# A written instruction order that ends with the first unit is continued to the end of the second

## The chip, the cores and the metric

The kernel runs on one core of a Trainium2 chip. Its engines have queues of their own, each worked off in order: PE (TensorE, matmuls and transposes), DVE (VectorE), ACT (ScalarE), POOL (GpSimd) and SP (SyncE, which here only issues DMA loads). The metric is the device time in microseconds (us). Three runs of the kernel before gave 574.34, 570.67 and 573.80 us, median 573.8.

## The reference

A windowed attention, a gated feed-forward layer and a layer of eight experts with a balanced assignment follow each other; 2 batches of 768 tokens, 8 heads of 64, model width 512:

```python
k_sum = k.reshape(B, H, nb, block, D).max(axis=3)      # block 32, nb 24
v_sum = v.reshape(B, H, nb, block, D).mean(axis=3)
scores_l = where(|i - j| < 16, scale * q @ k.T, -1e9)  # window
scores_s = scale * q @ k_sum.T + log(block)            # block means
a = softmax(concat([scores_l, scores_s]))
x = a @ concat([v, v_sum])

h = x @ w_in                                           # 512 -> 2048
x = (h * clip(h + 3, 0, 6) / 6) @ w_out                # 2048 -> 512
# then: logits x @ w_gate, each expert takes its 192 best tokens, relu(x @ w1) @ w2
```

## The kernel before

**Tiles and units.** The 1536 tokens are 12 tiles of 128; tiles 0 to 5 are batch 0 and 6 to 11 batch 1. Three tiles make a unit, so units 0 and 1 are batch 0, units 2 and 3 batch 1. A tile is worked on in two halves of four heads, numbered 0 to 23 (half 12 is the first of tile 6). The first layer's product of a unit is 16 slices (`gemm1_slice`, L684 to L686) of 12 matmuls of 384 columns each. Slices take turns in two PSUM banks (5 and 6), so a slice can start only when the slice two before it has been read out by ACT and DVE.

**One half of attention** goes through all engines: scores on PE (L423), mask and minimum on DVE (L433), exponentials on ACT (L439), norms on DVE (L443, L444), scaling on POOL (L448), transposes on PE (L470), their copy on ACT (L475), values on PE (L492). Behind a tile's second half stand its high part on ACT (L504) and its low part on DVE (L509). Per tile there are also the turning of the queries (PE L384, ACT L389) and the window of keys (DVE L406). Three buffers `Abuf` carry the halves, so about two are under way at once.

**Once per batch** the keys are turned into `kT` (for batch 1: six groups of four transposes, L368, each with a copy on ACT, L370, and a maximum over blocks on DVE, L371). The means of the values over blocks take POOL additions (L202 in three steps for batch 1, L209 for batch 0), a matmul (L217) and three copies (L221). The six key loads of batch 1 (256 KB each) go into four buffers `k1`, so the last two can be issued only when the first two groups have been turned.

**The weights** of the first layer arrive as 64-bit floats: a load of 512 KB per slice (L269), three integer operations on DVE (L295), a high part on ACT (L313) and a low part on POOL (L316).

**The order of the work.** `FIRST` is a list of short names written by hand, one per step, and `first_unit` runs them one after the other. The names that matter here are, by engine: PE: `K`/`Q` turn keys and queries of the start, `F` scores, `U` transposes, `V` values, `QP` turned queries, `M` means, `G` slices of unit 0, `N` filler matmuls on `ident`; DVE: `T` mask, `S` norms, `W` window, `c` weight conversion, `XL`; ACT: `E` exponentials, `C`, `X`, `H`, `EV` (read-out of a slice), `PL` (copies of the means); POOL: `P` scaling, `B` additions, `L` low weights; SP: `k`, `q`, `v`, `w`, `vw`, `kb`, `qq`, `vb` loads (the ones with `b` are batch 1's keys and values). Before, `FIRST` covers unit 0's slices and the attention of units 0 and 1 (tiles 0 to 5), and it ends there.

From then on `drive` mixes generators: for `u` = 1, 2, 3 it merges `gemm1(u)`, whose steps count 1950 each, with `attend_unit(u + 1)`, which draws steps from `halves()`; each stream moves in proportion to what it has done of its total (`ATTS[u + 1]` for the attention, spread over -0.02 to 0.92 of the stage). Before, `halves()` starts with tile 6: it issues the additions of batch 1's values, then all of `kprep`, the queries and the window, and then the halves. The stage of `u` = 1 ends when tile 8 is finished; by then the two fronts of tile 9 have also been issued, since halves lag by two.

The attention's share of a stage before, and the read-out of a slice, in the few lines:

```python
st = [[attend_unit(u + 1), ATTS[u + 1], -0.02, END[u]]]
drive([[gemm1(u), G1, 0, 1]] + st, soon)

p = gemm1_slice(u, f)
ACT.activation(T[u][:, f, :], p, AF.Relu, bias=three)
soon.append(partial(gate, T[u][:, f, :], p))
```

Of the kernel before, what the change touches and what calls it, by code (L numbers as in the profile page):

```python
# [12 lines left out]
OP = mybir.AluOpType  # L13
# [41 lines left out]
k00 k01 k10 k11 q0 q1 v0 w0 v1 vw0 w1 w2 w3 vw2 qq3 vw1 K001 K000 KE001 KR001 K010 KE000 KR000 K011 KE010 KR010  # L55
KE011 KR011 K100 KM0 K101 KE100 KR100 W0a KE101 K110 KR101 K111 KE110 KR110 KE111 Q01 KR111 Q00 QE01 KM1 W0b
QE00 Q11 Q10 QE11 F0 QE10 T0 E0 B0 N2 F1 T1 E1 S0 W1 P0 N3 M0 S1 c0_0 P1 c0_1 F2 B1 U0 c0_2 C0 T2 w4 qq4 H0 N1
U1 E2 F3 L0 M1 T3 C1 S2 W2 P2 E3 c1_0 F4 U2 PL2 c1_1 T4 C2 PL0 S3 N2 F5 c1_2 P3 PL1 W3 V0 U3 E4 T5 V1 c2_0 vw3
w5 X0 S4 c2_1 P4 E5 XL0 c2_2 N5 QP_3 C3 S5 H2 U4 c3_0 P5 H1 V2 c3_1 L2 C4 V3 c3_2 QE_3 U5 L1 X1 c4_0 V4 C5 XL1
F6 H3 c4_1 V5 L3 T6 QP_4 vw5 w6 w7 qq5 X2 E6 XL2 F7 c4_2 G0 W4 QE_4 H4 T7 L4 E7 G1 c5_0 S6 c5_1 P6 EV0 F8 EV1 S7  # L60
c5_2 P7 G2 T8 w9 w8 H5 E8 L5 c6_0 F9 c6_1 G3 EV2 W5 c6_2 U6 S8 EV3 c7_0 P8 H6 G4 T9 C6 L6 E9 c7_1 U7 c7_2 QP_5
w11 w10 EV4 S9 P9 C7 G5 c8_0 H7 c8_1 QE_5 L7 c8_2 U8 EV5 H8 c9_0 G6 L8 c9_1 c9_2 F10 EV6 w13 w12 vw4 H9 G7 T10
E10 L9 c10_0 c10_1 F11 EV7 S10 V6 c10_2 P10 G8 T11 w14 C8 H10 c11_0 E11 L10 c11_1 U9 c11_2 G9 EV8 S11 w15 kb0
kb1 kb2 kb3 qq6 vb0 vb1 H11 c12_0 P11 c12_1 L11 V7 EV9 c12_2 G10 vw6 qq7 C9 c13_0 H12 c13_1 X3 L12 c13_2 V8 EV10
# [34 lines left out]
def build(ctx, tc, q, k, v, w_in, w_out, w_gate, w1, w2, out):  # L99
# [30 lines left out]
    def bank(i):  # L130
        return psum.tile([128, 512], FT, name=f"bank{i}")
# [67 lines left out]
    def vsum(b):
        m = KR // 2  # L200
        while m:
            POOL.tensor_tensor(vs[:, :, :m], vs[:, :, :m], vs[:, :, m:2 * m], op=OP.add)  # L202
            m //= 2
# [7 lines left out]
    def vsum_mul(rows):  # L211
        means.append(bank(4))
        for i in rows:
            vsum_more(i, i == rows[0], i == rows[-1])

    def vsum_more(i, first, last):
        PE.matmul(means[-1][:KEYS], zones, vs[:, :, i], start=first, stop=last)  # L217

    def vsum_place(i):
# [87 lines left out]
        return win32[s % 4] if s < NF else wout32[(s - NF) % 3]  # L307

    def w_high(s):
        if s % 2 == 0:  # L310
            for _ in w_tiles(s):
                pass
        ACT.activation(WH[s], w_source(s), AF.Copy)  # L313

# [45 lines left out]
        ACT.activation(qT0[:, 2 * g + j].rearrange("p (s r) -> p r s", r=UT),  # L360
                       qps[g, j][:, :U].rearrange("p (r s) -> p r s", r=UT), AF.Copy)

    def kprep(b):
        for j in range(S // 128):
            x = raw.pop(("kraw", b, j))
            p = bank(2 + j % 2)
            for hp in range(HP):
                PE.transpose(p[:, hp * 128:(hp + 1) * 128],  # L368
                             x[:, 2 * hp:2 * hp + 2, :].rearrange("p h d -> p (h d)"), ident)
            ACT.activation(kT[:, :, :, 16 * j:16 * j + 16], p.rearrange("p (h s r) -> p h r s", h=HP, r=KR), AF.Copy)  # L370
            DVE.tensor_reduce(ks[:, :, 4 * j:4 * j + 4], p.rearrange("p (h n r) -> p h n r", h=HP, r=BLK),  # L371
                              axis=AX.X, op=OP.max)
            if b and j + 4 < S // 128:
                soon.append(partial(load_rows, "kraw", k, b, j + 4))
            yield 450
# [150 lines left out]
    pend, finished = [], set()  # L526

    def halves():
        for n in range(2 * UT, NT):
            b, i = divmod(n, 6)  # L530
            if i == 0:
                vsum(b)
                yield from kprep(b)
                q_prep(n)
                window(n)
                yield 2400
            for h in range(2):
                t = pend.pop(0) if len(pend) >= LAG else None
                if t:
                    turn(*t)  # L540
                    turned.append(t)
                    yield 660
                after = h == 1 and i < 5
                front(n, h, after)
                yield 1250 + 450 * after
                pend.append((n, h))
                while turned:
                    if turned[0] == (6 * b, 0):
                        vsum_mul([0])
                        for j in range(3):  # L550
                            vsum_place(j)
# [812 lines left out]
```

## Time and profile before

| | before |
|---|---|
| runs | 574.34, 570.67, 573.80 us |
| profiled execution, its own time | 573.23 us |
| its span, first to last instruction | 571.5 us |
| PE busy | 546.8 us, 96% |
| DVE, ACT, POOL busy | 360.7 (63%), 295.0 (52%), 168.1 us (29%) |
| start to the first slice of unit 0 | 0 to 41.1 us |
| unit 0's slices, with the attention of unit 1 | 41.1 to 85.6 us |
| unit 1's slices, with the attention of unit 2 | 85.6 to 146.3 us |
| unit 2's slices, with the attention of unit 3 | 146.3 to 191.1 us |
| the rest | 191.1 to 571.5 us |

The profiled time is 1.7 us longer than its span. Busy time counts an engine's own instructions. Matmuls overlap, so the time from one start to the next tells more of PE than the sum of their durations. A wait is put down to what released it.

### The profile page before, as it was taken

To read this page: it belongs to the slowest core of one execution; us is meant where nothing else is said; L and a number is where in the kernel's file an instruction comes from. 1 tells how busy PE (TensorE), PEld (TensorE's weight loads), DVE (VectorE), ACT (ScalarE), POOL (GpSimd) and SP (SyncE) were. 2 spreads that over 40 slices of the span, in tenths; PEclk is the share of its full clock that TensorE was granted. 3 is DMA by queue.
4 is the path that set the end of the run, shared out by engine and by line. 5 is a ranking of instruction groups with operands and counts; after the bars stand their busy time and mean duration, and the time that the engine had idled before them with its cause. 6 is when DMAs were issued, how large, how long until landed. Compare 5 with 4: busy or idle time off the path is not lost.

```text
span 571.5 us, 10909 instructions
## 1 busy us (share of the span) xinstructions
PE 546.8 (96%) x3901; PEld 459.8 (80%) x3901; DVE 360.7 (63%) x1036; ACT 295.0 (52%) x702; POOL 168.1 (29%) x198
## 2 busy tenths in 40 slices
PE   8889997899999999999999999998999999999993
PEld 8579896788989989866777777786888988998892
DVE  6799834445577786710165554543687888888870
ACT  4797643665544454732232322334567677676760
POOL 1646535112011232742254344463001110111011
PEclk9999998999999999999999999999999999999998
DMA  9996994122100453500070000025589987998701
GB/s 223 256 196 202 244 207 103 34 48 47 26 2 2 144 184 120 173 1 1 2 219 1 0 2 1 0 97 180 159 243 283 276 239 245 269 280 236 244 30 33
DMA packets 98271, 75.06 MB, mean 131 GB/s; under 512 B 38112, under 2 KB 84704, under 8 KB 98208
## 3 DMA queue, kind: packets, MB, share of 16 engines
q1 hardware_dynamic: 96224, 67.96, 44.0%
q0 software_dynamic: 1984, 6.32, 3.0%
q8 instruction: 33, 0.54, 0.4%
q14 instruction: 30, 0.25, 0.1%
HBM read 67.55 MB, written 6.71 MB: 130 GB/s over the span
## 4 chain that ended last, share of the span: by engine, by line
PE 56%; issue 27%; POOL 5%; DVE 4%; ACT 3%; DMA 2%; POOLq 0%; SPq 0%; DVEq 0%
PE bank L684 7%; PE bank L815 7%; PE bank L686 7%; PE bank L685 6%; PE bank L816 6%; PE bank L817 6%; POOL out_dram L1167 3%; PE bank L423 2%; PE bank L492 2%; POOL xs L748 2%; PE bank L726 2%; PE bank L470 2%; ACT A L439 2%; PE bank L638 1%; PE bank L335 1%
## 5 line engine op out<-in xcount | busy, mean ns | idle before, releaser
L684 PE MATMUL bank<-x,wh 128*128 128x384 f32 x256 | 91.6, 358 | 1.3 <-DVE t L714 1.3
L325 DVE TENSOR_TENSOR wl<-t,wh 128x1024 fp32r<-128x1024 f32 x64 | 77.0, 1221 | 20.5 <-ACT wh L324 18.7
L686 PE MATMUL bank<-x,wl 128*128 128x384 f32 x256 | 86.3, 337 | 0.0
L792 ACT ACTIVATE thx<-t 128x384 fp32r<-128x384 f32 (+2 forms) x80 | 36.0, 458 | 96.7 <-PE bank L816 89.3
L685 PE MATMUL bank<-x,wh 128*128 128x384 f32 x256 | 85.9, 336 | 0.0
L815 PE MATMUL bank<-wh,thx 128*128 128x512 f32 x192 | 79.4, 414 | 1.1 <-ACT thx L792 1.1
L793 POOL TENSOR_TENSOR tlx<-t,thx 128x384 fp32r<-128x384 f32 (+1 forms) x56 | 56.0, 1001 | 77.3 <-ACT thx L792 70.7
L817 PE MATMUL bank<-wh,tlx 128*128 128x512 f32 x192 | 75.4, 393 | 0.6 <-DVE tlx L793 0.5
L816 PE MATMUL bank<-wl,thx 128*128 128x512 f32 x192 | 75.0, 391 | 0.0
L1192 PE MATMUL bank<-x,wh 128*128 128x384 f32 x256 | 73.7, 360 | 0.5 <-DVE x L1118 0.5
L324 ACT ACTIVATE wh<-t 128x1024 fp32r<-128x1024 f32 x64 | 65.6, 1047 | 0.0
L1194 PE MATMUL bank<-x,wl 128*128 128x192 f32 x256 | 64.2, 251 | 0.0
L694 ACT ACTIVATE t<-bank,three 128x384 f32<-128x384 f32 x48 | 27.9, 581 | 65.4 <-PE bank L686 65.3
L1167 POOL DMA_INDIRECT out_dram<-t,idx x16 | 14.9, 931 | 141.5 <-DVE t L1216 136.0
L684 PEld LDWEIGHTS bank<-x,wh 128*128 128x128 f32 x256 | 48.3, 189 | 4.7 <-DVE t L714 2.2
L448 POOL TENSOR_TENSOR A<-A,sm 128x480 f32<-128x480 f32 x24 | 24.4, 1018 | 89.2 <-ACT at L475 41.9
L1194 PEld LDWEIGHTS bank<-x,wl 128*128 128x128 f32 x256 | 48.9, 191 | 0.3
L1192 PEld LDWEIGHTS bank<-x,wh 128*128 128x128 f32 x256 | 48.1, 188 | 1.2 <-DVE x L1118 0.8
L1208 PE MATMUL bank<-wh,t 128*128 128x512 f32 x128 | 48.9, 391 | 0.0
L685 PEld LDWEIGHTS bank<-x,wh 128*128 128x128 f32 x256 | 48.5, 189 | 0.0
L686 PEld LDWEIGHTS bank<-x,wl 128*128 128x128 f32 x256 | 48.2, 188 | 0.0
L815 PEld LDWEIGHTS bank<-wh,thx 128*128 128x128 f32 x192 | 36.0, 188 | 12.0 <-issue 2.9
(202 smaller groups left out, 1033.1 us busy)
## 6 DMA issues: line engine op xcount, KB each, us to landing
t<-in_moe_w_dram SPq DMA_DIRECT2D x128, 256.0 KB
t<-in_moe_w_in_dram SPq DMA_DIRECT2D x16, 512.0 KB
big<-in_moe_w_out_dram SPq DMA_DIRECT2D x16, 512.0 KB
VW<-in_v_dram SPq DMA_DIRECT2D x20, 192.0 KB
t<-in_v_dram SPq DMA_DIRECT2D x4, 768.0 KB
raw<-in_q_dram SPq DMA_DIRECT2D x9, 256.0 KB
t<-xs SPq DMA_DIRECT2D x8, 258.0 KB
t<-in_k_dram SPq DMA_DIRECT2D x4, 384.0 KB
```

Of the source, the lines that this page charges most:

```text
L324: ACT.activation(hi, x, AF.Copy)
L325: DVE.tensor_tensor(lo, x, hi.bitcast(FT), op=OP.subtract)
L684: PE.matmul(p, wh[:, kk, :], xh[:, kk, :], start=kk == 0, stop=False)
L685: PE.matmul(p, wh[:, kk, :], xl[:, kk, :], start=False, stop=False)
L686: PE.matmul(p, wl[:, kk, :], xh[:, kk, :], start=False, stop=kk == KD - 1)
L793: (DVE if placed[0] else POOL).tensor_tensor(ths[i][1], t, ths[i][0].bitcast(FT), op=OP.subtract)
L815: PE.matmul(acc[j], th[:, c], WH[s], start=f == 0, stop=False)
L816: PE.matmul(acc[j], th[:, c], WL[s], start=False, stop=False)
L817: PE.matmul(acc[j], tl[:, c], WH[s], start=False, stop=f == NF - 1)
L1192: PE.matmul(p, a[:, kk, :], xt[:, kk].rearrange("p c s -> p (c s)"), start=kk == 0, stop=False, skip_group_check=True)
L1194: PE.matmul(p[:, :CAP], b[:, kk, :], xt[:, kk, 0, :], start=False, stop=kk == KD - 1, skip_group_check=True)
L1208: PE.matmul(p, x, w, start=m == 0 and i == 0, stop=m == NM - 1 and i == 2)
```

## The change

`FIRST` goes on behind the last slice of unit 0. It now also holds unit 1's 16 slices (`Y`, read out by `YE` and gated by `GT`), batch 1's key groups (`KT` on PE, `KX` on ACT, `KN` on DVE), its means (`VS0` to `VS2` on POOL, `MB` on PE, `PB` on ACT), the queries of tiles 6 to 9, the halves 12 to 17, and the loads of tiles 6 to 11. Inside the part that was written before, many steps stand elsewhere too. `drive` begins at `u` = 2, and `halves()` at tile 9, with nothing under way, so the two fronts of tile 9 are issued there. Two of the eight filler matmuls at the start are gone. The sum of work is otherwise the same.

```diff
-ATTS = [0, 0, 26868, 18414]
+ATTS = [0, 0, 0, 21366]
 FIRST = """
...
+U11 VS0 G14 C11 V11 EV14 G15 X5 XL5 VS1 KT1 EV15 Y0 kb5 qq6 KN1 KX1 VS2 QP_7 YE0 KT3 GT0 KT0 KX3 KN3 Y1 kb4 vw8
+KX0 KN0 KT5 YE1 Y2 KN5 KX5 GT1 KT2 YE2 QP_6 KN2 KX2 Y3 qq8 qq9 QE_6 GT2 KT4 YE3 Y4 KN4 KX4 GT3 W6 MB YE4 GT4 Y5
+PB0 PB1 F12 PB2 Y6 T12 YE5 E12 GT5 F13 YE6 S12 QP_8 T13 P12 QE_7 Y7 E13 GT6 W7 S13 U12 YE7 P13 GT7 Y8 C12 F14
...
-    warm(8)
+    warm(6)
...
-    def kprep(b):
-        for j in range(S // 128):
...
+    def k_turn_rows(j):
+        x = raw.pop(("kraw", 1, j))
+        kps[j] = p = bank(2 + j % 2)
+        for hp in range(HP):
+            PE.transpose(p[:, hp * 128:(hp + 1) * 128],
+                         x[:, 2 * hp:2 * hp + 2, :].rearrange("p h d -> p (h d)"), ident)
+    def k_copy_rows(j):
+        ACT.activation(kT[:, :, :, 16 * j:16 * j + 16], kps[j].rearrange("p (h s r) -> p h r s", h=HP, r=KR), AF.Copy)
+    def k_max_rows(j):
+        DVE.tensor_reduce(ks[:, :, 4 * j:4 * j + 4], kps[j].rearrange("p (h n r) -> p h n r", h=HP, r=BLK),
+                          axis=AX.X, op=OP.max)
...
     def halves():
-        for n in range(2 * UT, NT):
-            b, i = divmod(n, 6)
-            if i == 0:
-                vsum(b)
-                yield from kprep(b)
-                q_prep(n)
-                window(n)
-                yield 2400
+        for n in range(3 * UT, NT):
+            i = n % 6
...
+        elif kind == "Y":
+            hps[i] = gemm1_slice(1, i)
+        elif kind == "YE":
+            if i == 0:
+                T[1] = tpool.tile([128, NF, U], FT, name="t")
+            ACT.activation(T[1][:, i, :], hps[i], AF.Relu, bias=three)
+        elif kind == "GT":
+            gate(T[1][:, i, :], hps.pop(i))
...
-    for u in range(1, NU):
+    for u in range(2, NU):
```

**PE, the turning of batch 1's keys.** Before, behind unit 1's first slice (the L686 and L684 rows are its last and the next slice's first matmuls), four of the six groups stand in a row:

```order
L686 MATMUL bank_1199<-x,wl 128x384
L368 MATMUL bank_1214<-ident,t 128x128 x4
L368 MATMUL bank_1222<-ident,t 128x128 x4
L368 MATMUL bank_1229<-ident,t 128x128 x4
L368 MATMUL bank_1236<-ident,t 128x128 x4
L684 MATMUL bank_1243<-x,wh 128x384
```

In the change (the slice's lines are now L674 to L676, the keys' line L367), at the same place:

```order
L676 MATMUL bank_1183<-x,wl 128x384
L384 MATMUL bank_1202<-ident,raw 128x128 x4
L367 MATMUL bank_1209<-ident,t 128x128 x4
L367 MATMUL bank_1215<-ident,t 128x128 x4
L674 MATMUL bank_1222<-x,wh 128x384
```

One group stands ahead of the first slice, the queries of tile 7 and two groups behind it (groups 3 and 0, whose loads need no buffer freed), and groups 5, 2 and 4 one each behind the second, third and fourth slice.

**SP, the queue of loads from the weights of the last slices on.** Before (L269 are weights, L180 with `in_k` batch 1's keys, L184 its values for the means, L192 windows of values, L180 with `in_q` queries):

```order
L269 DMA t<-in_moe_w_in_dram 128x4x256 x6
L192 DMA VW_95<-in_v_dram 96x8x64 x2
L269 DMA t<-in_moe_w_in_dram 128x4x256 x2
L180 DMA t<-in_k_dram 128x8x64 x4
L180 DMA raw<-in_q_dram 128x8x64
L184 DMA t<-in_v_dram 96x8x256 x2
L192 DMA VW_94<-in_v_dram 80x8x64
L192 DMA VW_94<-in_v_dram 96x8x64
L180 DMA raw<-in_q_dram 128x8x64
L192 DMA VW_95<-in_v_dram 96x8x64 x2
L192 DMA VW_96<-in_v_dram 96x8x64 x2
L180 DMA t<-in_k_dram 128x8x64 x2
```

In the change the first key load and half of the values stand between the weights (weights are still L269, keys and queries L185, values L189, windows L197):

```order
L269 DMA t<-in_moe_w_in_dram 128x4x256 x2
L185 DMA t<-in_k_dram 128x8x64
L197 DMA VW_95<-in_v_dram 96x8x64 x2
L269 DMA t<-in_moe_w_in_dram 128x4x256 x4
L189 DMA t<-in_v_dram 96x8x256
L269 DMA t<-in_moe_w_in_dram 128x4x256
L185 DMA t<-in_k_dram 128x8x64
L269 DMA t<-in_moe_w_in_dram 128x4x256
L197 DMA VW_96<-in_v_dram 96x8x64
L197 DMA VW_96<-in_v_dram 80x8x64
L269 DMA t<-in_moe_w_in_dram 128x4x256 x2
L197 DMA VW_94<-in_v_dram 80x8x64
```

and a little later the two key loads that wait for a buffer stand ahead of the windows `VW_96`, behind which both stood before:

```order
L189 DMA t<-in_v_dram 96x8x256
L197 DMA VW_95<-in_v_dram 96x8x64 x2
L185 DMA t<-in_k_dram 128x8x64 x2
L185 DMA raw<-in_q_dram 128x8x64
L185 DMA t<-in_k_dram 128x8x64
L185 DMA raw<-in_q_dram 128x8x64
L185 DMA t<-in_k_dram 128x8x64
L197 DMA VW_96<-in_v_dram 96x8x64 x2
```

**DVE, around the window of tile 2** (L406), in the start of the kernel. Before, it stands behind the mask of half 3 (`A_90`) and the norms of half 2:

```order
L433 ISA A_90,sm<-bank_383,mask 128x120
L433 ISA sm 128x1
L443 TENSOR_SCALAR sm<-sm 128x4
L444 RECIPROCAL sm<-sm 128x4
L406 COPY kw<-kT 128x4x96 x2
L295 TENSOR_SCALAR bank_411<-t 128x512
L295 SCALAR_TENSOR_TENSOR bank_411<-t,bank_411 128x512
L433 ISA A_91,sm<-bank_413,mask 128x120
```

In the change it stands between the mask of half 2 (`A_92`) and that of half 3 (`A_90`):

```order
L433 ISA A_92,sm<-bank_332,mask 128x120
L433 ISA sm 128x1
L295 SCALAR_TENSOR_TENSOR t<-t,bank_329 128x512
L406 COPY kw<-kT 128x4x96 x2
L433 ISA A_90,sm<-bank_365,mask 128x120
L433 ISA sm 128x1
L433 ISA A_90,sm<-bank_366,mask 128x120
L433 ISA sm 128x1
```

The scores of half 4 on PE read this window.

## Rows read from the trace of the kernel before

**Rows 1.** Busy time by stage: stretch, PE, PEld, DVE, ACT, POOL, PEclk, DMA share, GB/s.

```profile
0.00:41.10 41.10, 35.08 (x483) 27.74 (x483) 31.73 (x127) 28.54 (x82) 17.81 (x21) 1.00 1.01 225
41.10:85.60 44.50, 44.50 (x384) 41.01 (x382) 32.76 (x95) 27.68 (x84) 21.74 (x19) 1.00 0.91 218
85.60:146.30 60.70, 54.79 (x492) 48.57 (x490) 28.07 (x115) 34.86 (x104) 14.74 (x10) 0.97 0.28 61
146.30:191.10 44.80, 44.19 (x380) 40.51 (x378) 31.55 (x96) 19.82 (x58) 4.98 (x6) 1.00 0.07 25
```

**Rows 2.** PE in order of time: start, us, line, tiles, count, idle before.

```profile
1.74 3.78 PE L163 MATMUL bank<-ident 128*128 128x128 f32 x16 [1.74 <-DVE ident L142]
...
85.57 1.03 PE L368 MATMUL bank<-ident,t 128*128 128x128 f32 x8
...
87.49 0.34 PE L684 MATMUL bank<-x,wh 128*128 128x384 f32 x1
88.02 0.34 PE L684 MATMUL bank<-x,wh 128*128 128x384 f32 x1
...
93.57 1.98 PE L368 MATMUL bank<-ident,t 128*128 128x128 f32 x8 [4.00 <-DMA t<-in_k_dram]
```

**Rows 3.** Busy time in the stretch behind that wait, columns as in rows 1.

```profile
93.60:95.60 2.00, 2.00 (x9) 1.82 (x10) 0.27 (x1) 0.61 (x2) 0.00 (x0) 0.50 0.01 3
```

**Rows 4.** PE's groups from 41.0 to 85.5 us: count, busy us, mean ns, idle.

```profile
L492 PE MATMUL bank<-at,VW 120*64 120x64 f32 x96 | 4.1, 228 | 0.0
L470 PE MATMUL bank<-ident,A 128*120 128x128 f32 x24 | 3.6, 275 | 0.0
L423 PE MATMUL bank<-kw,qT 64*64 64x120 f32 x70 | 3.0, 274 | 0.0
L384 PE MATMUL bank<-ident,raw 128*128 128x128 f32 x4 | 0.6, 273 | 0.0
```

**Rows 5.** PE's groups from 85.5 to 146.2 us, with the waits before them.

```profile
L423 PE MATMUL bank<-kw,qT 64*64 64x120 f32 x128 | 5.3, 276 | 0.0
L470 PE MATMUL bank<-ident,A 128*120 128x128 f32 x27 | 4.3, 280 | 0.8 <-POOL A L448 0.8
L492 PE MATMUL bank<-at,VW 120*64 120x64 f32 x96 | 4.1, 228 | 1.1 <-ACT VW L221 1.1
...
L384 PE MATMUL bank<-ident,raw 128*128 128x128 f32 x20 | 3.2, 283 | 0.0
L217 PE MATMUL bank<-t,zones 96*120 96x512 f32 x2 | 1.0, 592 | 0.0
```

**Rows 6.** The chain that ended last: a half's exponentials, scaling left out, transposes.

```profile
134.03 1.51 ACT A L439 x8
...
137.16 0.65 PE bank L470 x4
```

**Rows 7.** DVE in order of time: mask of halves 0 and 3, a conversion.

```profile
15.78 0.28 DVE L433 CUSTOM_DVE_ANT_0 A<-bank,mask 128x120 f32<-128x120 f32 x1 [1.47 <-PE bank L423]
...
20.87 0.67 DVE L295 TENSOR_SCALAR bank<-t 128x512 int32<-128x512 int32 x1
...
24.65 0.28 DVE L433 CUSTOM_DVE_ANT_0 A<-bank,mask 128x120 f32<-128x120 f32 x1 [0.84 <-PE bank L423]
```

**Rows 8.** SP's queue in order of time: start, us, load, count.

```profile
82.14 7.00 SPq L192 DMA_DIRECT2D VW<-in_v_dram  x4
89.65 1.24 SPq L180 DMA_DIRECT2D t<-in_k_dram  x2
98.61 6.48 SPq L180 DMA_DIRECT2D raw<-in_q_dram  x2
```

**Rows 9.** Busy time while one query load lands, columns as in rows 1.

```profile
99.80:101.10 1.30, 1.30 (x21) 0.96 (x20) 0.00 (x0) 0.39 (x1) 0.00 (x0) 1.00 0.84 191
```

**Rows 10.** POOL's additions for batch 1, in order of time.

```profile
85.27 8.32 POOL L202 TENSOR_TENSOR t<-t 96x2048 f32<-96x2048 f32 x3 [6.24 <-DMA t<-in_v_dram]
```

**Rows 11.** Waits of PE from 146.2 to 191 us: total, times, longest.

```profile
PE bank L684 <- DVE t L714: 0.6, 2, 0.3
```

More of the change, by code (lines that the diff above doesn't have):

```diff
@@ L54 @@
 FIRST = """
[L55 to L64, printed above, removed]
@@ L65 @@
-XL3 H13 G11 c14_0 L13 c14_1 c14_2 U10 EV11 G12 H14 c15_0 C10 L14 c15_1 c15_2 V9 EV12 H15 G13 vw7 X4 L15 XL4 V10
-EV13 U11 G14 C11 V11 EV14 G15 vw8 X5 XL5 EV15
+k00 k01 k10 k11 q0 q1 v0 w0 v1 vw0 w1 w2 w3 vw1 qq3 K000 K001 KE000 KR000 K010 KE001 KR001 K011 KE010 KR010 K101
+KE011 KR011 K100 KM0 KE101 KR101 K111 KE100 KR100 Q00 KE111 KR111 W0a Q01 QE00 K110 QE01 Q10 KR110 KE110 KM1 Q11
+QE10 W0b F0 QE11 B0 T0 E0 N2 F1 T1 E1 N1 M0 S0 W1 P0 c0_0 F2 S1 B1 U0 c0_1 C0 T2 E2 c0_2 N2 F3 P1 w4 vw2 qq4 M1
@@ new lines @@
+W2 H0 T3 L0 E3 U1 c1_0 F4 S2 c1_1 P2 C1 S3 PL2 c1_2 N2 U2 P3 PL0 T4 c2_0 C2 N2 F5 E4 V0 c2_1 U3 T5 V1 E5 c2_2 S4
+c3_0 P4 X0 S5 C3 c3_1 P5 PL1 N5 U4 XL0 c3_2 QP_3 C4 W3 V2 qq5 w5 vw3 w6 w7 kb0 H1 H3 U5 L1 c4_0 QE_3 V3 c4_1 C5
+F6 L3 vw4 X1 c4_2 V4 H2 XL1 w8 V5 H4 L2 T6 QP_4 X2 F7 E6 XL2 L4 T7 G0 E7 W4 c5_0 QP_5 EV0 S7 G1 c5_1 P7 QE_4 S6
+c5_2 P6 H5 F8 EV1 L5 G2 c6_0 T8 E8 c6_1 F9 c6_2 G3 EV2 S8 w10 w9 H6 c7_0 P8 QE_5 W5 L6 U6 EV3 c7_1 G4 C6 T9 E9
+c7_2 w11 vb1 U7 EV4 c8_0 G5 C7 S9 c8_1 P9 H7 c8_2 L7 F10 EV5 w12 kb1 H8 G6 T10 E10 L8 c9_0 c9_1 F11 EV6 S10 G7
@@ L67 @@
+PB0 PB1 F12 PB2 Y6 T12 YE5 E12 GT5 F13 YE6 S12 QP_8 T13 P12 QE_7 Y7 E13 GT6 W7 S13 U12 YE7 P13 GT7 Y8 C12 F14
+YE8 GT8 V12 T14 Y9 E14 S14 F15 YE9 P14 GT9 U13 QE_8 W8 Y10 C13 T15 E15 V13 YE10 U14 vw9 qq10 S15 P15 X6 GT10 F16
+C14 XL6 Y11 T16 E16 U15 YE11 S16 V14 P16 C15 GT11 F17 QP_9 T17 E17 Y12 W9 QE_9 S17 U16 P17 YE12 Y13 GT12 C16 V15
+YE13 GT13 U17 vw10 X7 XL7 V16 C17 Y14 V17 YE14 GT14 Y15 vw11 qq11 X8 XL8 YE15 GT15
 """
@@ L197, in vsum_load, with vsum @@
         load_first(vs, v, b, slice(0, H), RH[g], KR)
[L199 to L203, printed above, removed]
+    def vsum(i):
+        m = KR // 2 >> i
+        POOL.tensor_tensor(vs[:, :, :m], vs[:, :, :m], vs[:, :, m:2 * m], op=OP.add)
     means = []
@@ L209, in vsum_halve, with vsum_mul @@
         POOL.tensor_tensor(vs[:, :, lo:lo + 2], vs[:, :, lo:lo + 2], vs[:, :, lo + 2:lo + 4], op=OP.add)
[L211 to L216, printed above, removed]
+    def vsum_mul(i, first, last):
+        if first:
+            means.append(bank(4))
         PE.matmul(means[-1][:KEYS], zones, vs[:, :, i], start=first, stop=last)
@@ L309, in w_high @@
     def w_high(s):
-        if s % 2 == 0:
-            for _ in w_tiles(s):
+        if s not in WH:
+            for _ in w_tiles(s // 2 * 2):
                 pass
@@ L361, in q_copy_first @@
                        qps[g, j][:, :U].rearrange("p (r s) -> p r s", r=UT), AF.Copy)
-    def kprep(b):
-        for j in range(S // 128):
[L365 to L375, printed above, removed]
+    def k_turn_rows(j):
[9 more added lines that the diff above has]
+                          axis=AX.X, op=OP.max)
     XH, XL, xps = {}, {}, {}
@@ L547, in halves @@
                 while turned:
[L548 to L551, printed above, removed]
                     values_then(*turned.pop(0))
@@ L847, in build, with first_units @@
     hps = {}
-    def first_unit(x):
+    def first_units(x):
         kind = x.rstrip("0123456789_")
@@ L897, in first_unit @@
         elif kind == "M":
-            if i == 0:
-                means.append(bank(4))
             for j in range(2):
-                vsum_more(4 * i + j, i == j == 0, i == j == 1)
+                vsum_mul(4 * i + j, i == j == 0, i == j == 1)
+        elif kind == "KT":
+            k_turn_rows(i)
+        elif kind == "KX":
+            k_copy_rows(i)
+        elif kind == "KN":
+            k_max_rows(i)
+        elif kind == "VS":
+            vsum(i)
+        elif kind == "MB":
+            vsum_mul(0, True, True)
+        elif kind == "PB":
+            vsum_place(i)
         elif kind == "PL":
@@ L933, in build @@
     for x in ORDER:
-        first_unit(x)
+        first_units(x)
     second = gemm2()
     tlast = late = None
-    for u in range(1, NU):
+    for u in range(2, NU):
         st = []
```

3 lines of the change are left out of this document (added).

## The prediction

> **What bounds the kernel now.** I read the busy time by stage first [rows 1]. PE is busy for all 44.5 us of the stage of unit 0's slices and for 44.19 of the 44.80 us of unit 2's: there the matmuls set the time. In unit 1's stage PE is busy for 54.79 of 60.70 us, and at a granted clock of 0.97 instead of 1.00. Up to 41.1 us it is busy for 35.08, with DMA share 1.01. DVE and ACT are far from full in all three later stages. So the written order can win only where PE waits: in unit 1's stage, and in the start.
>
> Next, PE in order of time [rows 2]. The key groups of batch 1 begin at 85.57 us; after one slice two more follow, and the last two wait 4.00 us for their load. They then take 1.98 us instead of 1.03. The granted clock tells why: 0.50 in the 2.0 us behind that pause, the lower of its two levels, 1.2 instead of 2.4 GHz [rows 3]. Over the stage the clock's 0.97 [rows 1] amounts to 0.03 x 60.7 = 1.8 us of lost work. PE's groups in that stage name two more waits, 1.1 us for the copies of the means and 0.8 us for POOL's scaling [rows 5]. Together 4.0 + 1.8 + 1.1 + 0.8 = 7.7 us.
>
> The same from the other side. Two L684 starts, three matmuls apart, lie 0.53 us apart [rows 2], so a slice of 12 takes 2.12 us and sixteen 33.9. Beside them unit 0's stage holds 4 halves of scores (16 rows each; the other 6 of the 70 belong to a half begun before it), 6 of values (16 each), 6 of transposes (4 each) and 1 turning of queries (4) [rows 4]: 17 pieces in 44.5 - 33.9 = 10.6 us, 0.62 us each. Unit 1's stage holds 8 halves of scores, 6 of values, 7 of transposes (the seventh runs over the end) and 5 turnings of queries [rows 5], 26 pieces, 16.1 us, six key groups at 0.5 (1.03 for two), 3.1 us, and the means, 1.0 us: 33.9 + 16.1 + 3.1 + 1.0 = 54.1. It took 60.7, so 6.6 us were waits. I use 6.6, the smaller of the two.
>
> **The change, part by part.**
>
> *Unit 1's stage.* The key groups now stand one to three at a time with slices between them. Group 5, the first that needs a freed buffer, stands behind two slices, the queries and two groups: 2 x 2.12 + 0.62 + 2 x 0.5 = 5.9 us after group 1, whose end frees its buffer. A query load of the same 256 KB, alone, is issued at 98.61 [rows 8] and has moved by 101.1 us [rows 9], 2.5 us. Before, the two key loads were issued at 89.65, behind 7.0 us of window loads in SP's queue [rows 8], and landed together by 93.57, 3.9 us. Both are under 5.9 us, so if SP's queue is free the wait is gone, and with it the pause that halves the clock. Before group 5 the queue holds everything that it held before the old ones but one window pair and one query load (384 + 256 KB, 2.9 us at 218 GB/s), so it should be. The means stand behind the fifth slice, so POOL's additions (8.32 us [rows 10]) have five slices, six groups and two turnings, 5 x 2.12 + 3.1 + 1.2 = 14.9 us, and the copies of the means lie under the next slices: that wait goes too. From a half's exponentials to its transposes the chain needs 3.1 us [rows 6], and the mask before them about 1 us (four steps of 0.28, overlapping [rows 7]). The written order gives a half, from its scores to its transposes, at least two slices and two pieces, 2 x 2.12 + 2 x 0.62 = 5.5 us.
>
> So the stage loses its 6.6 us of waits. I give 0.6 us back for waits that a fixed order across three engines will bring anew, as much as unit 2's stage has with its gate [rows 11]. Bounds: 0 and 4 us. Four pieces (two score halves, a transpose, the queries of tile 10) leave it for unit 2's stage, 2.5 us: 60.7 - 6.6 - 2.5 + 0.6 = 52.2 us.
>
> *Unit 2's stage* takes those four pieces: 44.8 + 2.5 = 47.3. DVE (31.55) and ACT (19.82 us) have room for the masks and exponentials that come along [rows 1], so they cost PE's time alone. Its attention now starts with nothing under way; slices fill the first steps. The moved work is worth nothing either way.
>
> *The start.* DVE's queue decides when the first slice can go, since its last need is tile 2's low part. Three things differ. Four filler passes fewer: 16 take 3.78 us [rows 2], so keys can be turned up to 0.9 us earlier, and DVE's first mask, which waits 1.47 us for scores [rows 7], comes between nothing (if the key loads decide) and 0.9 us earlier; I take 0.6, since PE waited for no key load at the start. The window of tile 2 stands ahead of half 3's mask and is copied while PE makes the scores that DVE waited 0.84 us for [rows 7]: that wait goes. And one conversion operation more, 0.67 us [rows 7], stands ahead of tile 2's low part. Net 0.6 + 0.84 - 0.67, about 0.8 us earlier. Against it, POOL's second addition for batch 0 now stands ahead of half 1's scaling, and with it that half's transposes come later; the scores of half 4 stand behind them, and DVE has the window, a mask and three conversions to do meanwhile. Bounds: 2 us earlier (both waits of DVE, 1.47 + 0.84, gone, 0.67 spent, and some on ACT), 1 us later.
>
> What the fillers do to the clock can't be read from its row, which says 1.00 throughout, though the first 16 passes start 0.24 us apart (3.78 us over 16 [rows 2]); the eight transposes of two key groups, also 128 columns each, take 1.03 us, half as much a piece. If the pace rises after a number of passes, 0.9 us is won; if it rises at a fixed time, the keys run 0.9 us longer at half pace and about half is won, and the sum is 0.2 to 0.3 us off either way. The Trainium skill, "TensorE: Matmul & The Clock Gate", Part 1, says that warming up is a budget of time and not a number of matmuls; by it the sum would be 566.6 us instead of 566.4.
>
> *Loads between the weights.* The first key load, half of the values and another key load (256 + 768 + 256 KB, 5.9 us at 218 GB/s) now stand ahead of the last weights. In unit 0's stage DMA is at 0.91 and PE waited for nothing [rows 1], and these bytes were moved in that stage before, only later. I cost it at nothing; if the weights had no lead, 5.9 us would show as waits ahead of the last slices.
>
> **Sum.** Against the profiled execution: 573.2 - 0.8 (start) - 6.6 + 0.6 (unit 1's stage) +- 0 (the moved pieces) = 566.4 us. It is 0.6 us under the median of the three runs, so the same sum on the median would give 567.0; I predict 566.4.
>
> **The rivals.**
>
> *Half of it.* The loads of the keys come late again, or the start does not shorten. If SP is as busy with the windows ahead as it was until 89.1 us [rows 8], load 5 lands near 93.5 again; group 5 is due 5.9 us after group 1, which ends near 85.3: 91.2 us. That is a wait of 2.3 us. With the start unchanged (0.8) and 1 us more of gate waits: 566.4 + 4.1 = 570.5 us. For it: DMA at 0.91 to 1.01 up to 85.6 us [rows 1]; the values for the means landed only at 85.27 [rows 10]. Against it: fewer bytes stand ahead.
>
> *More of it.* All 7.7 us of named waits go, nothing returns, the start gives 2 us: 573.2 - 9.7 = 563.5 us.
>
> *Slower.* The order ties PE to DVE and ACT. A slice needs its bank read out and gated, and the gates now stand at fixed places among masks, windows and norms in DVE's queue. Unit 2's stage shows the price of one such wait, 0.3 us, twice [rows 11]. If each of the 14 slices that reuse a bank in unit 1's stage waited, the gain of 6.8 us would be gone from 0.5 us each on, and at 0.9 us each 14 x 0.9 = 12.6 us make 566.4 + 12.6 = 579 us. Against it: DVE had 28 of 60.7 us of work in this stage and ACT 35 [rows 1]; in 52 us they stay under 70%.
>
> **How the numbers follow.** Forecast (564.5 to 568.4) 0.55, more of it 0.12, half of it 0.26, slower 0.07. A measurement of this kernel can hardly tell 1% (5.7 us, 568.1 us) from no change, the three runs themselves lying 3.7 us apart. Faster by over 1%: forecast and more, 0.66. Within 1%: half of it and a little of the forecast, 0.27. Slower 0.07. The range reaches from a little under "more", 562.5, to a little over "half", 571.0; it leaves out the slower case, some of "half" and a little below, under 0.2 together.
>
> **What would show it.** Unit 1's stage at about 52 us with no row of PE waiting for `in_k` and the clock at 1.00; unit 2's at 47; the first slice at about 40.3 us; everything behind as long as it was. Wrong would be: a wait of key group 5 for its load, gate waits (L704) in many slices, or a first slice later than 41.1.

## The result, and the profile after

| | before | after |
|---|---|---|
| median time (six runs each) | 573.64 us (570.67 to 574.86) | 565.88 us (565.03 to 567.08) |
| ratio to before, 95% interval | | 0.9875 [0.9844, 0.9906] |
| profiled execution | 573.23 us | 566.29 us |
| its span | 571.5 us | 564.5 us |

The change is faster by 1.25%, 0.5 us from the 566.4 us forecast. A second timing of it beside other kernels (e8 below) gave 0.9879 [0.9852, 0.9905].

Busy time by stage after, in the order of [rows 1] (stretch; its length; busy us and instructions of PE, weight loads, DVE, ACT, POOL; granted clock; DMA share; GB/s): the start, unit 0's slices, unit 1's, unit 2's, the rest.

```profile
0.00:43.30 43.30, 36.41 (x480) 27.80 (x480) 33.77 (x128) 28.92 (x84) 18.21 (x22) 0.92 1.00 215
43.30:87.80 44.50, 44.50 (x383) 40.78 (x381) 33.25 (x93) 27.97 (x81) 26.17 (x20) 1.00 1.02 222
87.80:138.80 51.00, 51.00 (x468) 46.24 (x467) 25.01 (x95) 32.19 (x87) 9.07 (x8) 1.00 0.32 63
138.80:185.90 47.10, 45.98 (x405) 41.68 (x402) 34.66 (x116) 23.36 (x75) 5.92 (x6) 1.00 0.06 11
185.90:564.50 378.60, 367.72 (x2174) 302.20 (x2172) 236.59 (x604) 184.37 (x377) 108.83 (x144) 0.99 0.45 138
```

Unit 1's stage went from 60.7 to 50.9 us (the row is cut at round times). PE is busy for all of it, at a clock of 1.00 where it was 0.97. Unit 2's stage took over some work and some waits, 44.8 to 47.1. The start is longer, 43.3 against 41.1 us, at a clock of 0.92, and the rest is shorter, 378.6 against 380.4.

The keys of batch 1 on PE after, in order of time (start, us, line and tiles, count); these answer to the L368 rows of [rows 2]:

```profile
87.93 0.60 PE L367 MATMUL bank<-ident,t 128*128 128x128 f32 x4
88.28 0.42 PE L674 MATMUL bank<-x,wh 128*128 128x384 f32 x1
...
90.45 0.60 PE L384 MATMUL bank<-ident,raw 128*128 128x128 f32 x4
90.89 1.04 PE L367 MATMUL bank<-ident,t 128*128 128x128 f32 x8
...
93.86 0.60 PE L367 MATMUL bank<-ident,t 128*128 128x128 f32 x4
...
96.40 0.60 PE L367 MATMUL bank<-ident,t 128*128 128x128 f32 x4
...
99.36 0.60 PE L367 MATMUL bank<-ident,t 128*128 128x128 f32 x4
```

No row names a wait ahead of it. Group 5 starts at 93.86, 5.6 us after the group whose buffer its load needed (88.28, where the next slice begins). SP's queue shows that load issued as soon as the buffer was free; it answers to the 89.65 row of [rows 8]:

```profile
88.56 0.37 SPq L185 DMA_DIRECT2D t<-in_k_dram  x1
88.97 0.58 SPq L185 DMA_DIRECT2D raw<-in_q_dram  x1
91.95 0.37 SPq L185 DMA_DIRECT2D t<-in_k_dram  x1
```

### The profile page after: what moved, and what is told of

Same layout as the page of the kernel before. It is cut to its first block, busy times and chain, and to the rows that moved or that the text cites. A ratio compares the mean times of both kernels' runs of the same rounds, so it can differ in the third digit from the quotient of the medians.

```text
span 564.5 us, 10892 instructions
## 1 busy us (share of the span) xinstructions
PE 545.6 (97%) x3899; PEld 458.7 (81%) x3899; DVE 363.3 (64%) x1036; ACT 296.8 (53%) x702; POOL 168.2 (30%) x198
## 4 chain that ended last, share of the span: by engine, by line
PE 58%; issue 27%; DMA 5%; DVE 4%; POOL 4%; ACT 1%; SPq 1%; POOLq 0%; DVEq 0%
PE bank L805 8%; PE bank L674 8%; PE bank L806 7%; PE bank L807 7%; PE bank L676 7%; PE bank L675 7%; POOL out_dram L1175 3%; DMA t<-in_v_dram 2%; PE bank L492 2%; PE bank L423 2%; PE bank L716 2%; PE bank L470 2%; PE bank L628 1%; DMA big<-in_moe_w_out_dram 1%; PE bank L1041 1%
## 5 line engine op out<-in xcount | busy, mean ns | idle before, releaser
L674 PE MATMUL bank<-x,wh 128*128 128x384 f32 x256 | 91.8, 359 | 0.8 <-DVE t L704 0.8
L325 DVE TENSOR_TENSOR wl<-t,wh 128x1024 fp32r<-128x1024 f32 x64 | 77.0, 1221 | 20.4 <-ACT wh L324 18.1
L676 PE MATMUL bank<-x,wl 128*128 128x384 f32 x256 | 86.1, 336 | 0.0
L674 PEld LDWEIGHTS bank<-x,wh 128*128 128x128 f32 x256 | 48.0, 188 | 4.3 <-issue 1.6
L676 PEld LDWEIGHTS bank<-x,wl 128*128 128x128 f32 x256 | 48.0, 188 | 0.0
L807 PEld LDWEIGHTS bank<-wh,tlx 128*128 128x128 f32 x192 | 36.0, 188 | 9.2 <-DVE tlx L783 1.2
```

The lines of the kernel that those rows point to most:

```text
L325: DVE.tensor_tensor(lo, x, hi.bitcast(FT), op=OP.subtract)
L674: PE.matmul(p, wh[:, kk, :], xh[:, kk, :], start=kk == 0, stop=False)
L676: PE.matmul(p, wl[:, kk, :], xh[:, kk, :], start=False, stop=kk == KD - 1)
L807: PE.matmul(acc[j], tl[:, c], WH[s], start=False, stop=f == NF - 1)
```

## The experiments

The kernel before took 573.2 us beside e1 to e4, 573.7 beside e5 to e8 and 575.4 beside e9 to e11, so ratios are compared. Each expectation stands as it was written ahead of the run. The table has the stages of one profiled execution each, in us.

| kernel | median us | ratio [95%] | start | unit 0 | unit 1 | unit 2 | rest |
|---|---|---|---|---|---|---|---|
| before | 573.64 | 1 | 41.1 | 44.5 | 60.7 | 44.8 | 380.4 |
| e9, before again | 574.90 | one run | 43.1 | 44.5 | 60.2 | 44.8 | 380.5 |
| e10, before, third | 575.21 | one run | 41.4 | 44.5 | 62.4 | 44.8 | 380.4 |
| the change | 565.88 | 0.9875 [0.9844, 0.9906] | 43.3 | 44.6 | 50.9 | 47.1 | 378.6 |
| e8, the change again | 566.91 | 0.9879 [0.9852, 0.9905] | 44.3 | 44.6 | 50.9 | 47.1 | 378.9 |
| e1, old start | 569.54 | 0.9916 [0.9882, 0.9950] | 44.1 | 44.5 | 53.3 | 47.0 | 379.0 |
| e2, new start alone | 569.28 | 0.9922 [0.9889, 0.9956] | 42.6 | 44.6 | 57.0 | 44.8 | 378.0 |
| e4, spread alone | 566.90 | 0.9880 [0.9824, 0.9936] | 42.4 | 44.6 | 55.2 | 44.8 | 378.2 |
| e11, spread and new start | 569.25 | 0.9887 [0.9870, 0.9903] | 43.8 | 44.6 | 54.6 | 44.8 | 380.3 |
| e5, key groups in a row | 569.38 | 0.9924 [0.9897, 0.9951] | 43.5 | 44.6 | 53.9 | 47.1 | 378.6 |
| e3, eight more fillers | 565.59 | 0.9849 [0.9800, 0.9899] | 41.7 | 44.6 | 50.9 | 47.1 | 378.9 |
| e6, eight fillers at the start | 566.41 | 0.9881 [0.9848, 0.9914] | 43.7 | 44.6 | 50.9 | 47.1 | 378.9 |
| e7, means later | 566.23 | 0.9881 [0.9857, 0.9905] | 43.1 | 44.6 | 50.9 | 47.1 | 378.5 |

### The change's two halves: e1 and e2

e1 keeps the order of before, its loads included, up to the last slice of unit 0, and goes on as the change does:

```diff
-k00 k01 k10 k11 q0 q1 v0 w0 v1 vw0 w1 w2 w3 vw1 qq3 K000 ...
+k00 k01 k10 k11 q0 q1 v0 w0 v1 vw0 w1 w2 w3 vw2 qq3 vw1 K001 ...
...
-... EV14 G15 X5 XL5 VS1 KT1 EV15 Y0 kb5 qq6 ...
+... EV14 G15 vw8 X5 XL5 EV15 VS0 VS1 KT1 Y0 kb5 ...
-    warm(6)
+    warm(8)
```

> The order of before up to the end of unit 0, unchanged (eight fillers at the start), followed by the new order of unit 1's stage. Theory: the gain lies in the continuation alone and the new order ahead of it costs 2.2 us (first slice at 43.3 instead of 41.1). Then first slice at 41.1, unit 1's stage 51, unit 2's 47 us, and about 563.7 us. Rival: the continuation needs the loads as the new first part places them; with the old one the key groups wait again, unit 1's stage is 53 to 56 us, and the time is 566 to 569 us.

e2 is the other half: the kernel before with the change's order up to that slice, unit 1 from the generators.

```diff
-... KR110 KE111 Q01 KR111 ... vw8 X5 XL5 EV15
+... QE10 W0b F0 QE11 ... X5 XL5 EV15 qq6 vw8
-    warm(8)
+    warm(6)
-        if s % 2 == 0:
-            for _ in w_tiles(s):
+        if s not in WH:
+            for _ in w_tiles(s // 2 * 2):
```

> The new order up to the end of unit 0 (six fillers), followed by the stages of before, with the key groups bunched and the loads of the second batch's remaining queries and values at the end of the written order. Theory: the first slice comes at 43 us and unit 1's stage keeps its waits, so 574 to 576 us, slower than before by 1 to 2 us. Rival: loads placed earlier are what frees unit 1's stage, whatever its order; then its wait for keys is gone and the time is 568 to 571 us.

PE's waits in unit 1's stage (engine, line, what for; us in total, times, longest), first of e1, then of e2:

```profile
PE bank L367 <- DMA t<-in_k_dram: 1.0, 1, 1.0
PE bank L384 <- DMA raw<-in_q_dram: 1.0, 1, 1.0
```

```profile
PE bank L368 <- DVE ks L371: 1.5, 2, 1.1
PE bank L492 <- ACT VW L221: 1.1, 1, 1.1
PE bank L470 <- POOL A L448: 0.8, 2, 0.5
```

With the old loads the new order waits 2.0 us for a key load and a query load, and its stage is 2.4 us longer than the change's. With the new loads the old order no longer waits for a key load at all: what stands between its groups in a row is DVE, whose maxima free the banks. Both rivals held, e1's time being half a microsecond above its rival's range. e1's first slice, expected at 41.1 us with the old start, came at 44.1 (more on this below). The gain isn't the continuation's alone: units 1 and 2 together take 100.3 us in e1 and 101.8 in e2, against 105.5 before and 98.0 in the change. Both halves work on the same key wait, so the two savings, 5.2 and 3.7 us, don't add up; together they give 7.5.

### One edit that spreads the groups, e4, and with the early loads, e11

e4 is the kernel before, with a higher count behind the fourth group, so that two slices stand between it and the last two; the attention's total is raised by the same 4550:

```diff
-ATTS = [0, 0, 26868, 18414]
+ATTS = [0, 0, 31418, 18414]
...
-            yield 450
+            yield 5000 if j == 3 else 450
```

> The kernel before with one edit: the attention stream counts 5000 instead of 450 behind the fourth key group, so two slices stand between it and the fifth. Theory: the 4.0 us of waiting for the load and the 1.8 us that the clock lost go and nothing else changes; unit 1's stage takes 55 us, the time is 568 us. Rival: the keys come later, so the halves behind them are squeezed and wait for each other; unit 1's stage is 58 us or more and the time 571 us or more.

e11 has this edit in e2.

> The kernel before with two parts of the change and not the third: the new start with its earlier key loads, and the one edit that spreads the last two key groups; the attention of unit 2 still comes from the generators. The edit alone left 55.2 us in unit 1's stage, and named waits of 1.1 us for the copies of the means, 0.9 for a mask and 0.2 for a key load. Theory: once the groups are spread the earlier loads have nothing left to save but the 0.2; units 1 and 2 together take 99.5 to 100 us against 98.0 in the change, whose written order gains its last 2 us by putting the means behind the fifth slice; about 566.5 to 567. Rival: early loads save in every order, as they do for the old generators (3.7 us); then units 1 and 2 together take 98 us or less, and the time is that of the change or below, 565.

PE's waits in unit 1's stage, of e4 and then of e11:

```profile
PE bank L492 <- ACT VW L221: 1.1, 1, 1.1
PE bank L423 <- DVE sm L433: 0.9, 1, 0.9
PE bank L368 <- DMA t<-in_k_dram: 0.2, 1, 0.2
```

```profile
PE bank L492 <- ACT VW L221: 1.1, 1, 1.1
PE bank L423 <- DVE sm L433: 0.9, 1, 0.9
```

The key wait in the two later profiles of the kernel before, e9 and e10, where it was 4.0 us in the first [rows 2]; unit 1's stage took 60.2 and 62.4 us in them:

```profile
PE bank L368 <- DMA t<-in_k_dram: 3.3, 1, 3.3
```

```profile
PE bank L368 <- DMA t<-in_k_dram: 5.5, 1, 5.5
```

The edit takes this wait to 0.2 us, and with it the slow clock behind it: unit 1's stage takes the 55 us expected, 5.5 less than in the first profile of before. That is nearly three quarters of what the change gains in units 1 and 2, from one edit of two numbers. By its time e4 can't be told from the whole change at all (0.9880 against 0.9875), but its profile has 2.2 us of the gain in the rest, which nothing here explains (below). e11 shows that the early loads then have next to nothing left to save (99.4 us for the two units, against 100.0), as the theory said. The last 1.4 us to the change's 98.0 go with the copies of the means (1.1) and one mask (0.9), both waits that the change doesn't have; it has 0.5 us more of others in unit 2's stage (below). e11's time of 569.25 is above the expected 567; its ratio, on the 573.64 us of the first runs, makes 567.2, and its profile has 380.3 us in the rest, where e4's has 378.2 (below).

### The groups in a row again: e5

The change, with the last three groups behind the first slice:

```diff
-KT3 GT0 KT0 KX3 KN3 Y1 kb4 vw8 KX0 KN0 KT5 YE1 Y2 ... KT2 ... KT4 YE3 Y4
+KT3 GT0 KT0 KX3 KN3 kb4 vw8 KX0 KN0 KT5 KT2 KX5 KN5 KX2 KN2 KT4 KX4 KN4 Y1 YE1 Y2 ...
```

> The changed kernel with batch 1's key groups bunched again: all but the first stand between unit 1's first and second slice, everything else as in the change. Group 5 is then due 3.8 us after group 1 instead of 5.9, group 4 some 1 us after group 0 whose buffer it needs, and each copy of a group (0.6 us) stands between two groups of one bank. Theory: PE waits 3 to 5 us there and the clock falls, unit 1's stage takes 55 us instead of 51, about 570 us. Rival: earlier loads alone are enough; 1 us or less is lost, 566 to 567 us.

PE in order of time, with the wait ahead of a row in brackets:

```profile
91.07 1.04 PE L367 MATMUL bank<-ident,t 128*128 128x128 f32 x8
93.08 1.25 PE L367 MATMUL bank<-ident,t 128*128 128x128 f32 x8 [0.98 <-DVE ks L374]
95.75 0.66 PE L367 MATMUL bank<-ident,t 128*128 128x128 f32 x4 [1.42 <-DVE ks L374]
```

The stage is 3.0 us longer, where 4 were expected, and the median 2.5 us above e8's of the same group of runs. The clock stayed at 1.00 in this stage, where a fall was expected. The wait named is 2.4 us for DVE's maxima, not for a load: even groups are turned into one bank and odd ones into another, so a group waits for the readers of the last one of its kind. With a slice between them those readers lie under the slice. So the spread has a use of its own beside the load's time.

### The start: e3, e6, e7, e9, e10

In the change PE stands still ahead of the means of batch 0 and its clock falls. Three edits in the start:

```diff
 e3
-E1 N1 M0 S0
+E1 N9 M0 S0
 e6
-    warm(6)
+    warm(8)
 e7
-E1 N1 M0 S0 W1 P0 c0_0 F2 S1 B1 U0 c0_1
+E1 N9 S0 W1 P0 c0_0 F2 S1 B1 U0 M0 c0_1
```

> The changed kernel with nine filler matmuls instead of one ahead of the first means of batch 0, so that PE does not stand still while POOL adds. Theory: the granted clock stays at 1.00 up to the first slice, which comes at about 41.3 us, and the time is about 563.8 us. Rival: the first slice is set by DVE's queue and the clock's fall costs nothing; then the time stays at 565.9 us.

> The changed kernel with eight filler matmuls at the very start instead of six. The changed kernel waits 0.8 us for a key load behind its third group, so the earlier start is partly lost there. Theory: no difference, within 0.5 us of the changed kernel (565.9 us). Rival, the prediction's term: 0.6 us slower, 566.5 us.

> The changed kernel with the first matmuls of batch 0's means moved behind the scores and the transposes that stood behind them, and nine fillers instead of one ahead of the scores. The values for the means land between 15.3 and 17.3 us from one profile to the next, and where they land late PE waits 1.7 to 2.4 us and the clock falls to 0.50 for some 5 us. Theory: the wait and the fall go, the first slice comes at 41 us or before, and the time is 1.5 to 2.5 us under that of the changed kernel in the same job, about 564 us. Rival: DVE's queue sets the first slice whatever PE does; then no difference, 565.9 us.

> The changed kernel itself, once more, for a second profile and for times beside the others of this job. All theories: 565 to 567 us, unit 1's stage 51 us, unit 2's 47 us; the first slice between 41 and 44 us, by when the first values land.

And two more profiles of the kernel before:

> The kernel before, profiled a second time, to see how far its start and its rest vary by themselves. Its first profile reached unit 0's first slice at 41.1 us, with the granted clock at 1.00 and the first POOL addition at 15.76 us; six profiles with the new start reached it at 41.7 to 44.3. Theory: the spread of the start (when the first values land, whether PE pauses long enough for the clock to fall) belongs to every kernel of this family, and 41.1 was at its lucky end; then this profile starts its first slice somewhere from 41 to 44 us, with the stages of units 0, 1 and 2 at 44.5, 60.7 and 44.8 again. Rival: the changed start is later by its order; then the kernel before lies at 41.1 again, within 0.3 us, and its clock stays at 1.00. The rest: 378 to 379 us if the first profile's 380.4 was its own, 380.4 again if the new order shortens it.

> The kernel before, profiled a third time, on the same two theories as the second look: by the one its first slice comes anywhere from 41 to 44 us, by the other at 41.1 within 0.3 us. The stages of units 0, 1 and 2 at 44.5, 60.7 and 44.8 us by both.

None of the three edits can be told from the change by its time: 565.59 with 0.9849 [0.9800, 0.9899], 566.41, and 566.23 beside 566.91. The 1.5 to 2.5 us expected of the later means didn't come. In the profiles of e3 and e7 the granted clock is 1.00 up to the first slice, as expected, which came at 41.7 and 43.1 us. In e7 PE was no longer held by the addition but by the windows and masks of DVE. In e3 the addition began early (15.30 us), so what its fillers did can't be told from that.

The change after, PE and then POOL and DVE, in order of time:

```profile
16.91 0.49 PE L168 MATMUL bank<-ident 128*128 128x128 f32 x2
19.26 3.77 PE L217 MATMUL bank<-t,zones 96*120 96x512 f32 x4 [1.86 <-POOL t L212]
22.96 1.08 PE L423 MATMUL bank<-kw,t 64*64 64x120 f32 x16
```

```profile
16.86 2.34 POOL L212 TENSOR_TENSOR t<-t 96x1024 f32<-96x1024 f32 x1 [14.68 <-DMA t<-in_v_dram]
```

```profile
17.76 1.48 DVE L443 TENSOR_SCALAR sm<-sm 128x4 f32<-128x4 f32 x1
19.27 0.18 DVE L444 RECIPROCAL sm<-sm 128x4 f32<-128x4 f32 x1
...
24.63 0.28 DVE L433 CUSTOM_DVE_ANT_0 A<-bank,mask 128x120 f32<-128x120 f32 x1 [2.12 <-PE bank L470]
```

Busy time in stretches of 2 us, columns as above (the clock is the third number from the end):

```profile
16.00:18.00 2.00, 1.33 (x18) 0.99 (x18) 1.19 (x11) 1.91 (x11) 1.14 (x1) 1.00 1.10 250
18.00:20.00 2.00, 0.74 (x1) 0.47 (x2) 1.97 (x4) 0.89 (x6) 1.61 (x2) 0.71 1.13 229
20.00:22.00 2.00, 2.00 (x4) 0.65 (x2) 1.97 (x5) 0.00 (x0) 0.69 (x1) 0.50 1.38 180
22.00:24.00 2.00, 2.00 (x19) 0.74 (x17) 0.52 (x1) 0.00 (x0) 1.69 (x1) 0.50 1.13 233
24.00:26.00 2.00, 2.00 (x20) 1.84 (x20) 1.37 (x9) 0.89 (x4) 1.60 (x2) 0.59 1.09 353
```

The values for batch 0's means let POOL begin its addition at 16.86 us; PE waits 1.86 us for it, the clock falls from 1.00 to 0.50, its lower level, and four matmuls take 3.77 us. DVE then waits 2.12 us for the next scores. In e8 the values came early, at 15.90 us, and another thing went wrong:

```profile
16.02 2.45 DVE L409 COPY kw<-ks 128x48 f32<-128x48 f32 x2
```

```profile
15.90 2.43 POOL L212 TENSOR_TENSOR t<-t 96x1024 f32<-96x1024 f32 x1 [13.71 <-DMA t<-in_v_dram]
```

These two small copies take 0.28 us in the change's other profile, and here they end 0.14 us after POOL's addition. The mask behind them is late, then PE, 2.33 us, and the clock falls again. The copies came 1.1 us later than in the other profile because the keys were turned more slowly. From 5 to 7 us PE is busy all the time in both, with 50 matmuls in the change's first profile and 26 in e8:

```profile
5.00:7.00 2.00, 2.00 (x50) 2.00 (x48) 0.56 (x1) 0.98 (x2) 0.00 (x0) 1.00 1.02 259
```

```profile
5.00:7.00 2.00, 2.00 (x26) 2.00 (x28) 0.00 (x0) 0.46 (x1) 0.00 (x0) 1.00 1.08 227
```

In all thirteen profiles PE's first matmul starts at 1.7 us and the matmuls run at half pace at first, though the granted clock of these stretches says 1.00. The pace rises at 5.7 to 7.6 us in the five profiles with the old start, at 5.1 and 6.3 in the change and e2, and at 10.1, 10.6 and 11.2 in e8, e11 and e5, which have the same start. In these three DVE's first mask comes at 18.1 to 18.4 us, in the ten others at 14.7 to 16.1. Whether two fillers fewer make the late rise likelier stays open.

The first addition of the three profiles of before starts at 15.76, 17.36 and 16.64 us, and of the change's at 16.86 and 15.90: that varies by itself. Five profiles have the order of before up to the first slice (before, e9, e10, e1, e4). They reached it at 41.1, 43.1, 41.4, 44.1 and 42.4 us, 42.4 on average. Five have the order of the change (its own two, e2, e5, e11): 43.3, 44.3, 42.6, 43.5 and 43.8, 43.5 on average. So 41.1 was at the lucky end, as the theory had it, though e10 lies within the rival's 0.3 us of it. The new start is 1.1 us later on average, with ranges that overlap. How much of that the new order causes stays open, and so does the part of the clock: e5 kept it at 1.00 and came at 43.5 us.

### The rest

The rest was 380.4, 380.5 and 380.4 us in the three profiles of before and 380.3 in e11, and 378.0 to 379.0 in all nine others, e2 and e4 among them, whose instructions there are those of before. ACT in the second layer's product, e10 and then the change:

```profile
393.70 0.31 ACT L792 ACTIVATE thx<-t 128x128 fp32r<-128x128 f32 x1 [1.63 <-PE bank L816]
395.16 0.31 ACT L792 ACTIVATE thx<-t 128x128 fp32r<-128x128 f32 x1 [1.15 <-PE bank L816]
```

```profile
385.10 0.95 ACT L782 ACTIVATE thx<-t 128x128 fp32r<-128x128 f32 x3
386.42 0.31 ACT L782 ACTIVATE thx<-t 128x128 fp32r<-128x128 f32 x1 [0.37 <-DVE tlx L783]
```

At one place ACT and DVE stand still for 1.1 to 2.5 us at a time in the four, and PE waits 1.1 to 1.6 us behind them; in the others they don't. The matmul named as the releaser had long been done; it was its signal that came late. By the trace's record of semaphore updates PE signals every 0.2 to 0.6 us at this place in the nine; in the four there are gaps of up to 1.4 to 2.6 us and then six updates within 0.2 us, the first of them just ahead of ACT's next operation. Why the signals are late in some kernels and not in others stays open, and so does whether the change has a part in these 1.8 us; no run was made for it.

## Why the prediction was right, and where it wasn't

**Unit 1's stage: the mechanism was right, two terms were off.** Forecast 52.2 us, measured 50.9. The key wait, the half clock behind it, the copies of the means and POOL's scaling are gone, as the steps said; group 5 was due after 5.6 us where 5.9 had been worked out, and its load was in time. One term mis-sized is the work moved: three pieces left the stage, not four, since the first of tile 9's two score halves still stands ahead of unit 2's first slice (138.80 us):

```profile
138.23 0.64 PE L423 MATMUL bank<-kw,qT 64*64 64x120 f32 x16
...
141.10 0.64 PE L423 MATMUL bank<-kw,qT 64*64 64x120 f32 x16
```

At 0.62 us a piece that is 1.9 us instead of 2.5. The other is the waits: of 7.7 us by name and 6.6 by subtraction the sum took the smaller, and the stage lost 60.7 - 50.9 - 1.9 = 7.9. The subtraction gave 54.1 us of work, less 1.9 moved 52.2; the stage is 1.3 shorter than that with PE always busy, so its unit prices were too high. The 0.6 us given back for new waits didn't come in this stage, nor did one gate wait (L704).

**Unit 2's stage: right, in part by luck.** 47.3 forecast, 47.1 measured in both profiles of the change. The moved work was 0.6 us smaller, and where PE had waited 0.6 us for the gate [rows 11] it now waits 1.1 us for two other engines:

```profile
PE bank L492 <- ACT at L475: 0.6, 1, 0.6
PE bank L470 <- POOL A L448: 0.5, 1, 0.5
```

**The start: wrong.** The step was "about 0.8 us earlier"; it came 2.2 us later in the profiles set against each other, and 1.1 on average over five each. Two things were missed. The base was one profile, whose 41.1 us was the best of five with that start. DVE's first mask did come 0.6 us earlier, as taken (15.23 against 15.78 us), but the four other profiles of the old start have it at 14.8 to 15.2. And the step counted DVE's two waits as idle time to be taken away (1.47 and 0.84 us), while it gave POOL's addition and PE's clock no part: DVE's norm took 1.48 us beside the addition, and behind a pause of 1.86 us the clock stood at 0.50 for nearly 7 us. What each of these costs by itself isn't shown. The bound of 1 us later was too near. As to the fillers, the prediction weighed a pace that rises after a number of passes against one that rises at a fixed time. It is neither: the pace rose after 16 to 94 matmuls over the thirteen profiles, and at 5.1 and 10.1 us in two executions of the change itself. So the traces agree with the Trainium skill ("TensorE: Matmul & The Clock Gate", Part 1) that warming up is not a number of matmuls; a fixed budget of time from the first matmul they don't bear out.

**Loads between the weights: right.** Unit 0's stage was 44.5 us before and 44.6 after, with PE busy throughout.

**The rest: not foreseen.** "As long as it was" failed by 1.8 us, to the change's advantage.

Against the first profile: +2.2 (start), +0.1 (unit 0), -9.8 (unit 1), +2.3 (unit 2), -1.8 (rest) = -7.0 us, the difference of the spans. The forecast was -6.8. So it is luck that the total is nearer than its parts: the start was 3.0 us worse than forecast, unit 1's stage 1.3 and the rest, of unknown cause, 1.8 us better.

**The rivals.** "Half of it" named a late key load; e1 shows that a wait comes back with the old loads, 1.0 us for a key load and 1.0 for a query load, so it was a real risk that the new loads avert. "More of it" had the waits right (all 7.7) and the start wrong. "Slower" fell: no gate of unit 1's slices was waited for, with DVE at 25.0 and ACT at 32.2 of 51.0 us.

## What to carry to other kernels

Look first whether one wait carries the gain: where a step needs a load that a buffer holds back, placing other work between can be worth most of what rewriting the order gains (here 5.5 of 7.5 us), and a spread, an earlier load and a new order don't add up where they remove the same wait. A wait of PE can cost more than its length: behind the 4.0 us for the key load the clock stood at 0.50 [rows 3], while behind e5's waits of 0.98 and 1.42 us it stayed at 1.00. Take several profiles of the kernel before where the sum rests on its start: here three differed by 2 us, over twice the 0.8 us that was forecast.

## What the runs showed of the hardware

The first profile of before has the same places of the start undisturbed, PE, POOL and DVE:

```profile
18.47 1.88 PE L217 MATMUL bank<-t,zones 96*120 96x512 f32 x4
```

```profile
15.76 2.35 POOL L209 TENSOR_TENSOR t<-t 96x1024 f32<-96x1024 f32 x1 [13.57 <-DMA t<-in_v_dram]
```

```profile
18.63 0.17 DVE L443 TENSOR_SCALAR sm<-sm 128x4 f32<-128x4 f32 x1
```

DVE operations between SBUF tensors stood still beside a POOL operation. DVE's norm of 128x4, 0.17 us there, behind the addition, took 1.48 us beside POOL's addition and ended at 19.24, 0.04 us after it; in e8 the two copies of 0.28 us took 2.45. The masks, which read a PSUM bank, kept their 0.90 us a half beside the same addition (the first began at 15.78 [rows 7], while POOL added from 15.76 to 18.11). The Trainium skill, "SBUF — State Buffer", section "SBUF: two separate sides", says that in some of its operations DVE shares a pair of ports with POOL, that whichever starts first holds it for its whole instruction, and that the other is blocked meanwhile. The traces agree as to DVE; of POOL they show little, since its additions took 2.34 to 2.60 us throughout.

PE's clock fell from 1.00 to 0.50 behind a pause of 1.86 us in a start that had kept it busy, and the first matmuls behind it ran at half pace (3.77 us against 1.88 for the same four). The length of the pause alone doesn't tell: the clock fell behind one of 1.33 us in e6 and stayed at 1.00 behind one of 1.73 in e5.

The same load, first values for the means, let POOL begin anywhere from 15.1 to 17.4 us over the thirteen profiles, though SP's order up to that load is the same. With the old start the first slice came later where POOL began later: 15.76, 16.64, 17.23, 17.29 and 17.36 us went with 41.1, 41.4, 42.4, 44.1 and 43.1. With the new start it didn't follow: 15.10, 15.40, 15.90, 16.34 and 16.86 us went with 43.5, 43.8, 44.3, 42.6 and 43.3.
